# Loads, engines and a new written-out order for the first groups of an attention and mixture-of-experts kernel

## The chip, the cores and the metric

One core of a Trainium2 chip runs the whole program: TensorE (PE), VectorE (DVE), ScalarE (ACT), GpSimd (POOL) and the DMA queues that SyncE (SP) and ScalarE issue. The metric is device microseconds of one launch. Three runs of the kernel before took 917.5, 918.54 and 920.09 us, median 918.54 us; the execution that was profiled took 916.3 us.

## The reference

`q`, `k` and `v` are 8 batches of 12 heads, 448 tokens of 64 elements each, in f32. Attention output is turned to 3584 tokens of 768 and goes through a mixture of 8 experts.

```python
q_n = q / sqrt(mean(q*q) + 1e-6) * g_q          # k_n likewise with g_k
scores = q_n @ k_n.T / 8
attn = softmax(scores)                          # the row maximum subtracted first
x = (attn @ v) as [3584, 768]
logits = x @ w_gate                             # then tokens to experts, greedily by logit, 448 each
out[tokens of e] = relu(x[tokens of e] @ w1[e]) @ w2[e]
```

## The kernel before

The 96 heads are worked in 24 groups of four heads. A group is 14 blocks of 128 rows for q and as many for k. Every f32 value that TensorE multiplies is split into a high and a low f16 half, so that a product is three matmuls.

For a group g the steps, by the names of the functions that the profile's lines belong to, are: load q and k (`load_qk`, lines 227 and 235 for the first three groups, 252 for the others); square on ScalarE (`square`, L301); sums of squares on VectorE (`sumsq`, L307); 1/sqrt in three steps (`rsqrt`: Ln on ScalarE, L313; Exp on ScalarE, L315; then a correction called the root, on VectorE in three small operations, L324 to L326, or on GpSimd in four, L318 to L321); q times the product of the two gains (`gain`, L368 or L371); q and k times 1/sqrt (`norm`, L342); the high half (`hi`, ScalarE, L376); the low half, value minus high half (`lo`, L379); transposes of both halves; a first product of high halves for the row maxima (`max_score`, L504 and L507, TensorE, and `max_reduce`, L514, VectorE); the maxima turned into a row (`put_max`, `rows_first`, `row_first`, L520 to L432); the scores (`scores`, L535 to L544), exp (L550, ScalarE) and attention times v (`av`, L569).

Groups 0 and 1 (`EARLY = 2`) go half by half, a = 0 (blocks 0 to 3) and a = 1 (blocks 4 to 6), and are transposed on TensorE (L402) and copied out of PSUM by VectorE (k's part, L410) and ScalarE (q's part, L412). From group 2 on a whole group goes at once and a DMA transposes it (L389). The tables `FIRST` and `ENG` say which engine does a step: "D" is VectorE, "P" GpSimd; a key such as `normk1` holds for half 1 of that group alone.

`load_qk(0, n)` for group 0: n = 0 to 3 is q, n = 4 to 7 is k. Parts 0 and 4 bring 192 KB (first heads of each pair), 1, 2, 5 and 6 bring the 32 KB tails, and 3 and 7 the other 192 KB. Half 0 needs the first three of these, half 1 the fourth. `load_qk(1, n)` and `load_qk(2, n)`: 0 to 2 is q (384 KB and two tails), 3 to 5 is k. Loads of group 0's k go on ScalarE's queue, all others on SyncE's. DMAs share eight completion semaphores: in the trace the first eight DMAs take one each, and each later one waits for the DMA that last had its semaphore.

What order the work has: `plan()` makes a list of 2117 tasks of the attention stage, each with its engine, and `ORDER` is a table of two characters for each task, written out, in which `Plan.run` emits them. Every engine and queue works through its own tasks in that order and waits where an operand isn't there. The routing and the experts come behind it and don't use the table.

Of the kernel before, what the change touches and what calls it, by code (L numbers as in the profile page):

```python
# [89 lines left out]
class Attention:  # L90
# [789 lines left out]
    def plan_first(self, plan, g, a):  # L880
# [51 lines left out]
        "3V3Y3W3X3a3bC7ROC83rME2S2q2T2r4A2sMGC9MF2UH5CACBCCRPMKH7CDCEMJMHMICF4BCG3s4C3tH6H83G2u2v202w1-2tRQRRH9HBHA3c4Y"
        "4ZCHCIHDRSHCHE3Z3d3u3w3v4a3y3H0D3I3JCJCKMLMNMRCL4DCM3x3+4E4F3KHFHGHHHICNCORTRUMMMOMQCPCQRV4cRW3z0E3-403L4G4HMP"
        "HJCRCSHL4KHKHMMSCTMTMYMWMX4dCUCVHN4bHOCWRXRYHPHQ3e3fMUCXRZCYHRMVCZ4eRaHS4fRb4I4L4J4M3gHVHTCaCbRc0FCcRd4NReMZMb"
        "MdCdHUHWRfCeRgMaHX4y4+CfCgMfMgMjCh4zCiMmMeMi4g4h414k4-Mc4O5K3lCjCkRhRiHZ5L4i4j4l3h3jHY3kHa4m3i0G4nHb4243444P4o"
        "MkClRjRkCmMhHd50HcCnRlCoMl4546He51525453RmRnHfCpCqRoHh4748HgHiMnCrRpCsHj4p49HlCtMsMtMrCuRqRvRuRyCvCwHkHm5M5O5N"
        "HnHpCxCyHo5PMoMpMqMu4Q4RS3Hr56HqHsCzS4C+11MyMvM+C-D0S5HtHxD1D2554S6658595A57MzMxMw4TD35QHu5RS65kS7S8S9D4SAHvHw"
        "Hy5mM-N5D5N4N3D6HzD75lD8N2H-4qSB4VSC4rH+I05n5o5p5S5T4U5W5U5V4WI15YI2D9DAN6N1N7NCDBDCN0SDI3I4685q5ZDDSEDESFNANB"
        "N8DFDGI5SGI6SHI7DHDIN9SISJRxRr67Rw5X5r5sI9DJDKSKI8IA5B4sIBICSLRzR+R-DLDMSMID6AIF5uIEIGRs5a4X6u6vDNDO69S0S15t5v"
        "4tNDNENH5C5DS2IHDPDQ6BNFNKNMDRNINGDS5w6W5xII6C4v4w6D6E6F4u6GIJDVNJILIKIMDWDTDUSNSOSPSQNNNPNQDXINIO5E5bIPIQDYDZ"  # L940
        "DaSRNLIR5yDbDc6X6H6I6K6LNONRNUNTSSSTRt4x5J5F6JIS5cIT5dSUSVDdDeSWNXIVDfNWNYNeDgNdDhNbNSNV5H6Y6ZIU6w6a6b5IIW5z6c"
        "6d5eDiDjSlSmDkSn5GIXIYIZDlDmSoSp6e6f0HNZNaNcDnIbIaSbSaId6gIc6yIe5f6hDo6xSqSr5+5-SsStNfNjNi6MDpDqIfIg5hIhDr6z7I"
        "6+6-70Ii6i6j72735g0I0JDsSuNlNgNhNkDtSvDuIjIkSc5jSdSeSfSgShSwSxSyDvDwIl7KImInSzDxSi5iSjDyNmNsNoDzNnNpNrNq7LD+D-"
        "S+S-E0Sk7g6k606NSXIp6l616462710KIoIrE1E2T0IqIsNtNuNw6O6P7JT1T2ItE3E4NyNxNvNzT3747M767N7O77757P7QN+O0E7T4E8T5Iv"
        "IuIwT6IxIy63E5E6O3N-O1E9T7EAIz65I+I-EBECO2O4T87RJ07iJ1T9TA6R6S6TJ2TBEDEEO5O7O66mTC6n7j7S6QJ3J47h6U7k78J5EFEGOC"
        "OEO8EHJ7O97UJ67V7TEIJ87l7mOAOBJ9EJSZ6VSYTHTI6oTK7WTRTSTTEK7nTUTVJBJAJCODOHENEOJDJF8486JEELEM85JGOJOGOOOIEPEQ87"
        "JHJIJJEROPOLESOFTWTXTYJL7A7BJK7o7q7p797sJNETEU7r7u7t0L7vTZJMJO8889TaTJ8S8T6p8A6s8B8C6qOMOKONTbTcEVEWTdJPJQ6rTL"
        "TNTMEXEYTeTfJRJTJSEbEcTOOQOVOUEZ8U8VEaJUTPTQ6t7CJXJVEd8D8W8s7XJW8E8GTGTE7w8IJY8FEeOXObOWEfOROTOdOS7D7EEg8X8Y8u"
        "8Z7GEhTgEiThJZJb7Y7ZTiOcEjEk8a8H8c8bJaTjJcTkOZOYOaTlElTmEmTn8vJdOeOgEnOjOkOhOfOiEo7FToJe7x8e8d8g8h8fTF7H7bTpEp"
        "TqTrEqJfJgJh7f7a9ETDErEsTsOlOrOnEtOqOoOmEu7yJiTtTu7zJj8t7+7c7e9GJkJlEvJm8w0M0NOsOpEwU79HOuOvExJnJoJpEyU8U97d8x"  # L950
        "UAJqEzOyE+UBOtOwOx0O8yE-UCF0UDUEJrJt9F9IJsJuUFF1F2OzP0O+P1F3UGF4JvJx8z8i8JTzU0T-T+83F5F68+8-0P9e9fJwJy0Q0R7-80"
        "9092P2O-P4P98K8L8MTx9JJz819KJ+J-F7F8P8P3P5P7UHUIUJK0UK9LF9FAULK1K3FBFC919M9NA0TyP6PA8N938O9OK2K49g8PU1U3U2UMUN"
        "UOFDFEK5K7UP82UQFFU4K6U5K8FGPBPEPGPHPDU69h9i9j9P8jFHFIPIPCPOFJA2A1A49QFKA3K98Q948RKAKB9SKCFLPFFMPNPJPLFNURUSUT"
        "UUFOKDKF8kUV8lTv958m9U9R8r9T0S0T0U0VPMPKUWUX0W0X8n8pKEKG8o9k0Y0Z0aFRFS0b9lKHKJKIKKFPUYFQPPPQPVFTFUKLKNUZUaUfUh"
        "KMFVFWPUPWPYFXKPKOKQFYKRKSFZFaPZKT8qKU96KV97TwUi9mKW9oAQ9nFbFcPcPXPSFdFeKXKYKZKa9qFhFiPRPTUpUqUrPaFfFg98KdKbUs"
        "UtFjFkPb9D9r999p9CKcKeA5UuUvA6A79BA80cAAABA90dPdPhPiPgFlKfKgFmUwUxKhKi9sFnFoUyPePjPfUz9W9XU+KjU-V0FpUgUjUlUkKl"
        "FqV1FrARFsUmPkPpPqPoPmUnUoFtFu0e9APrPnPwFvPxASATFwPlV29VACAEAF0fAD0gAoAq9YApAGV3V4AUAVAWKkKm9Z9aAXPsPtFxFyKn9d"
        "Uc9tV5V6KoKpFzF+PvPuV7Kr9uV8V99v9wUbUdAH9bKq9cKsKtF-ArG0PyQ2Q0P+G1AsVAVBKuG2KvKxG3G4AaKwAY0h0i0jAZAc0k0lKyAeUe"
        "Q1P-PzQ30mVCAtG5G6KzK+Q7Q9VDVEG7G89x0n0oAd0pAu9zVFAv9+VGVKVHK-L0AwAbAf9-VLVM9yL1L2BCBEAxAyAzG9GAQ5Q6QAQGGBGCBF"
        "L3L5L4GDGEQBQ8Q4QEQFVVVWVXL6VYAIL7L9L8AJAKAPVOGFBD0qVZQDGG0r0sQHQCALVaBGA+BHLAB0AOQIQJGHVbVcGILBLDVdVeLCLEGLGM"  # L960
        "QLQMQKGJGKAMA-BIBJB1BK0tQOQNQRQPGNLFLHVfVgVhViGOGPGQVjQTQQQUQSVkVlBMLGLIB2GRGSLJLLAgAhVmLKLMVNVPVRVQGTVJAiBLGU"
        "AjVnANVoLNBOLOAmLPLQGVGWVSQVQWQZGZGaLRLSVTLTGXGYQaQXQbVUGbGcLVLULWLXAlLYGdQYQcQiQhGeVpVqVrB3AnBQGfGgLZLbB4VsLa"
        "B5VtVIB6LcQgQfQeQdVuVvVwVxVyV-W1W3W2W4AkQjQnQkGhLd0u0vBN0w0x0yLeLfQmQoLgGiGjGkLjLhLiGnGoQpQlWBWCWDQqQrGlGmLkLl"
        "LnGpGqQuQwQsGrB7B9BAWEWFGsLmLoLpLrLqBSQtBTQvWJWKB8QxR0QyR1Q-Q+QzBPBRW0BUV+VzBBWLLtWMWSWTWNLsLuWULvW5W7W6LwWVWW"
        "BVLzLxX3W8W9WABYLyL+BXR2R6R7R3R5R4R8L-M1WGM0M2WaWbWcWdWeM5M3M4WHM6BWR9RFRERARCRBRGRLRKRJRDRMRIRHWjWkWlWrWsWtWm"
        "WnWOWQWuWPWXWfWhWYWvWIW-X0WRWxWoWZWgWiX1WpWqX2W+WyWzWw"
# [1031 lines left out]
```

## Time and profile before

| | us |
|---|---|
| median of three runs | 918.54 |
| profiled execution | 916.3 |
| its span, first to last instruction | 914.5 |
| PE busy in the span | 863.1 |
| DVE busy | 660.6 |
| ACT busy | 466.9 |
| POOL busy | 343.0 |

The profile page lists busy time by engine, a strip of 40 slices, the chain of work that ended last, and the costliest groups of instructions. The trace answers further questions: busy time of each engine in any stretch, waits by engine and releaser, and the instructions of a stretch in order of time.

### The profile page before, as it was taken

What the parts mean: (1) busy time and instruction counts of PE and PEld (TensorE: products, weight loads), DVE (VectorE), ACT (ScalarE), POOL (GpSimd) and SP (SyncE); (2) the same over time, 40 slices, a digit from 0 to 9 for tenths busy, and PEclk for the clock granted to TensorE, in tenths of its full rate; (3) what the DMA queues carried; (4) which work ended last, traced back from release to release, by engine and by line L of the source; (5) the groups of instructions that cost most, each with busy time, mean ns of one, the idle gap of its engine ahead of it and who ended that gap; (6) DMA issues with size and microseconds to landing.
All of it is one profiled execution on the core that took longest, in us unless ns stands there. A gap on an engine that the chain in (4) does not pass through costs nothing.

```text
span 914.5 us, 30177 instructions
## 1 busy us (share of the span) xinstructions
PE 863.1 (94%) x13219; PEld 579.4 (63%) x13220; DVE 660.6 (72%) x1465; ACT 466.9 (51%) x670; POOL 343.0 (38%) x433
## 2 busy tenths in 40 slices
...
GB/s 198 113 157 173 183 261 156 219 179 224 205 230 182 210 203 143 114 82 63 253 86 251 182 190 268 150 282 91 298 88 282 142 219 258 155 130 69 131 18 44
DMA packets 224952, 157.31 MB, mean 172 GB/s; under 512 B 162100, under 2 KB 211508, under 8 KB 224820
## 3 DMA queue, kind: packets, MB, share of 16 engines
...
q8 instruction: 103, 1.69, 0.7%
q10 hardware_dynamic: 834, 0.46, 0.2%
...
## 4 chain that ended last, share of the span: by engine, by line
PE 71%; issue 17%; DVE 5%; POOL 3%; DMA 2%; ACT 1%; SPq 1%; POOLq 0%; DVEq 0%
PE po L569 18%; PE ph L1775 16%; PE py L1792 13%; PE psc L535 9%; PE pm L504 4%; PE psc L537 3%; PE py L1801 2%; DVE mx L514 2%; POOL out_dram L1808 1%; POOL rows L1712 1%; DMA kqh<-s 1%; PE psc L542 1%; PE rp L1318 1%; DVE st L307 1%; PE rp L1475 1%
## 5 line engine op out<-in xcount | busy, mean ns | idle before, releaser
L514 DVE TENSOR_REDUCE mx<-pm 128x2 f32<-128x896 f32 x162 | 176.7, 1091 | 49.2 <-PE pm L504 44.8
L569 PEld LDWEIGHTS po<-v,e 128*64 128x64 f32 x5376 | 166.8, 137 | 31.8 <-issue 28.9
L569 PE MATMUL po<-v,e 128*64 128x65 f32 x5376 | 182.6, 223 | 2.9 <-issue 2.8
L1775 PE MATMUL ph<-xt,w1h 128*128 128x448 f16 (+2 forms) x708 | 183.5, 343 | 0.4 <-DVE xt L1733 0.3
L550 ACT ACTIVATE e<-psc 128x896 f32<-128x896 f32 x168 | 148.6, 912 | 49.9 <-PE psc L537 39.3
L1808 POOL DMA_INDIRECT out_dram<-y,idx x32 | 34.4, 1075 | 307.9 <-ACT y L1794 279.3
L1792 PE MATMUL py<-w2h,hh 128*128 128x384 f16 x384 | 125.0, 326 | 0.0
L1792 PE MATMUL py<-w2h,hl 128*128 128x384 f16 x384 | 125.0, 326 | 0.0
L1792 PE MATMUL py<-w2l,hh 128*128 128x384 f16 x384 | 125.0, 326 | 0.0
L1775 PE MATMUL ph<-xt,w1l 128*128 128x448 f16 (+2 forms) x354 | 119.9, 343 | 0.0
L1792 PEld LDWEIGHTS <-hh 128*128 128x128 f16 x768 | 73.6, 97 | 45.6
L1775 PEld LDWEIGHTS <-w1h 128*128 128x128 f16 x708 | 64.7, 97 | 52.7 <-issue 1.5
L1764 ACT ACTIVATE hh<-ph 128x448 f16<-128x448 f32 x56 | 30.5, 544 | 125.8 <-PE ph L1775 122.7
L1794 ACT ACTIVATE y<-py 128x384 f32<-128x384 f32 x48 | 23.5, 490 | 116.2 <-PE py L1792 96.0
L1712 POOL DMA_INDIRECT rows<-xd,idx x32 | 31.0, 969 | 114.9 <-DVE idlo L1480 46.8
L1579 DVE SCALAR_TENSOR_TENSOR w2l<-stage,w2h 128x768 f16<-128x768 f32 x64 | 60.2, 951 | 8.6 <-ACT w2h L1575 8.6
L504 PE MATMUL pm<-kqh 64*64 64x448 f16 x588 | 56.7, 362 | 1.8 <-DMA kqh<-s 1.4
L535 PE MATMUL psc<-kqh 64*64 64x448 f16 x588 | 56.0, 353 | 0.8 <-issue 0.4
L537 PE MATMUL psc<-rowq,rowk 64*64 64x448 f16 x588 | 55.8, 349 | 0.7 <-issue 0.7
L1766 DVE SCALAR_TENSOR_TENSOR hl<-ph,hh 128x448 f16<-128x448 f32 x56 | 34.1, 617 | 30.9 <-ACT hh L1764 30.8
L307 DVE TENSOR_REDUCE st<-sq 128x14 f32<-128x910 f32 (+2 forms) x52 | 52.7, 1016 | 4.4 <-ACT sq L301 4.4
L535 PE MATMUL psc<-kql,kqh 64*64 64x448 f16 x588 | 55.4, 349 | 0.0
(301 smaller groups left out, 1620.8 us busy)
## 6 DMA issues: line engine op xcount, KB each, us to landing
...
```

What stands on the lines that cost most here:

```text
L307: self.nc.vector.tensor_reduce(self.stat(g, 0, a)[:, i], self.view(self.T["sq", g, i], a), axis=AX.X, op=OP.add)
L504: self.nc.tensor.matmul(o, mine, self.every(k, r, a), start=True, stop=True)
L514: self.nc.vector.tensor_reduce(m, p[r, :, :448], axis=AX.X, op=OP.max)
L535: mm(o, mine, self.every(q, r, n), start=i == 0, stop=False)
L537: mm(o, one[r, :64], self.every(row, r, n), start=False, stop=True)
L550: self.nc.scalar.activation(e, p[:, :, :448], AF.Exp, scale=scale)
L569: self.nc.tensor.matmul(po[o:o + 64, w], self.T["e", d][:, h, q:q + 64], self.v32[g % 2][:, h, 4 * a + d % 7 % 4], start=d == ds[0], stop= ...
L1579: self.later(0.93, lambda w=w: self.nc.vector.scalar_tensor_tensor(l[:, w], v[:, w], self.WS, h[:, w], op0=OP.mult, op1=OP.subtract), k, i)
L1712: nc.gpsimd.indirect_dma_start(out=g[:n, c, :], out_offset=None, in_=self.xd, in_offset=bass.IndirectOffsetOnAxis(ap=idx[:n, c:c + 1], axi ...
L1775: nc.tensor.matmul(p, a, b[:, o], start=st, stop=sp)
L1792: nc.tensor.matmul(p, a[:, f, s], b[:, f, o], start=st, stop=sp)
L1808: st = nc.gpsimd.indirect_dma_start(out=self.out, out_offset=bass.IndirectOffsetOnAxis(ap=self.router.out[k][:n, c:c + 1], axis=0), in_=y[ ...
```

## The change

Three entries of `FIRST` and the whole table `ORDER` are replaced.

```diff
-    FIRST = (dict(root="D", gain="P", normq="P", normk="D", normk1="P", lok="D", lok1="P", loq="D", loq1="P"),
-             dict(root="D", gain="P", normq="P", normk="P", lok="P", loq="P"), dict())
+    FIRST = (dict(root="D", gain="P", normq="P", normq0="D", normk="D", normk1="P", lok="P", loq="P"),
+             dict(root="P", gain="P", normq="P", normk="P", lok="P", loq="P"), dict())
     ORDER = (
-        "050204031506160z1718191A0+1B0708000-1C1E1G1c1F1H1d1I1J1e1K1f1L091g1h1i1N1D1b1M011P1R242122252326281k1j1O1Q2x2z"
...
+        "03060402010507080z151618170+000-1D191A1B1C1E1F1c1d1G1H1e1I1J1f1K1g1h1i091L1N1b1k1j1n1l1p1O1M1P1R1o1Q1m21232624"
...
```

In group 0 the low halves of half 0 (k and q) go from VectorE to GpSimd, and q's norm of half 0 goes from GpSimd to VectorE. In group 1 the root of both halves goes from VectorE to GpSimd: three operations on VectorE become four on GpSimd, for each half. All else keeps its engine. The two tables, decoded by task number, begin so for each engine (x.y is group and half, h and l high and low half, "max 3.0" a block of the first product):

```
SP before:   q0 part 0, part 1, g_q, part 2, part 3, k1 main, q1 main, q1 tail, k1 tail, q1 tail, k1 tail, q2 main, ...
SP after:    g_q, q0 part 0, part 1, part 3, part 2, q1 main, q1 tail, k1 tail, k1 main, q2 main, k3, k1 tail, q1 tail, k2 main, q3, ...
ACT before:  load k0 part 4, 5, g_k, part 6, part 7, square q0.0, k0.0, q0.1, rsqrt 0.0 (2), square k0.1, rsqrt 0.1 (2), hi k0.0, hi q0.0,
             square q1.0, hi q0.1, square k1.0, hi k0.1, square q1.1, copy h0.0, ...
ACT after:   load g_k, k0 part 4, 5, 6, 7, square q0.0, q0.1, k0.0, k0.1, rsqrt 0.0 (2), rsqrt 0.1 (2), hi k0.0, hi q0.1, hi k0.1, hi q0.0,
             square q1.0, q1.1, k1.0, copy h0.0, copy h0.1, square k1.1, ...
DVE before:  ident, gains, sums q0.0, k0.0, q0.1, root 0.0, sums k0.1, norm k0.0, mask, root 0.1, lo k0.0, lo q0.0, copy h0.0, sums q1.0,
             k1.0, q1.1, copy l0.0, root 1.0, sums k1.1, max 0, max 1, root 1.1, copy h0.1, max 2, sums q2, max 3.0, ...
DVE after:   ident, gains, sums q0.0, q0.1, k0.0, k0.1, root 0.0, root 0.1, mask, norm k0.0, norm q0.0, sums q1.0, copy h0.0, sums q1.1,
             copy h0.1, sums k1.0, k1.1, max 0, max 3.0, max 2, copy l0.0, max 1, sums q2, copy l0.1, max 4, sums k2, row 0.0, ...
POOL before: gain 0.0, 0.1, norm q0.0, q0.1, k0.1, lo q0.1, k0.1, gain 1.0, 1.1, norm k1.0, q1.0, lo k1.0, norm q1.1, k1.1, lo q1.1,
             q1.0, k1.1, root 2, norm q2, k2, gain 2, lo k2, lo q2, ...
POOL after:  gain 0.0, 0.1, norm q0.1, k0.1, lo k0.0, q0.1, q0.0, k0.1, gain 1.0, 1.1, root 1.0, root 1.1, norm k1.0, q1.1, q1.0, lo q1.1,
             norm k1.1, lo q1.0, k1.0, root 2, lo k1.1, norm q2, k2, gain 2, lo k2, lo q2, ...
PE before:   transposes h0.0, l0.0, max 0, 1, 3.0, transposes h0.1, l0.1, max 2, 4, transposes h1.0, rows 0.0, max 3.1, 6, transposes h1.1, scores 0
PE after:    transposes h0.1, h0.0, max 3.0, 0, transposes l0.0, l0.1, max 1, 2, 4, rows 0.0, max 3.1, 6, transposes h1.0, max 5, scores 0
```

Further on the two tables hold the same tasks in nearly the same places on TensorE: the first score block of each group, counted in TensorE's 748 tasks, stands within eight places of where it stood. The DMA queue and GpSimd differ more. Of the 22 groups that a DMA transposes, the number whose high half is issued in the table with no reduction to spare before the first block that reads it is 11 before and 2 after.

## Rows read from the trace of the kernel before

**Rows 1.** Stretches: us; PE, PEld, DVE, ACT, POOL busy; clock; DMA share; GB/s.

```profile
0.00:19.30 19.30, 2.81 (x18) 1.95 (x18) 9.52 (x22) 8.55 (x18) 10.78 (x32) 1.00 0.72 203
19.30:45.00 25.70, 18.60 (x192) 10.01 (x194) 24.19 (x33) 19.04 (x39) 20.59 (x23) 1.00 0.41 118
...
100.00:400.00 300.00, 294.94 (x7547) 226.38 (x7541) 236.72 (x366) 220.60 (x326) 196.91 (x228) 1.00 0.96 194
```

**Rows 2.** What PE waited for, 0 to 60: us in total, times, longest.

```profile
PE po L402 <- ACT s L376: 9.5, 1, 9.5
PE pm L507 <- DVE mx L514: 5.9, 6, 3.0
```

**Rows 3.** First loads in order of time: start, us, engine; idle before in brackets.

```profile
4.06 0.46 SPq L235 DMA_DIRECT2D qkraw<-in_k_dram  x1
...
4.75 0.60 ACTq L227 DMA_DIRECT2D qkraw<-in_k_dram  x1
...
6.12 0.63 ACT L301 ACTIVATE sq<-qkraw 128x512 f32<-128x512 f32 x1 [4.10 <-issue]
...
10.04 1.05 ACT L301 ACTIVATE sq<-qkraw 128x512 f32<-128x512 f32 x2 [3.29 <-DMA qkraw<-in_k_dram]
```

**Rows 4.** Data rate in the first stretches, columns as in rows 1.

```profile
0.00:5.00 5.00, 0.08 (x1) 0.11 (x1) 0.51 (x2) 1.28 (x1) 3.17 (x23) 1.00 0.42 108
5.00:10.00 5.00, 0.58 (x2) 0.39 (x2) 0.92 (x2) 0.63 (x1) 2.22 (x2) 1.00 0.98 272
```

**Rows 5.** First group's operations in order of time, columns as in rows 3.

```profile
12.01 0.18 DVE L324 TENSOR_TENSOR st<-st 128x16 f32<-128x16 f32 x1
...
12.99 1.35 DVE L342 TENSOR_TENSOR kn<-qkraw,st 128x512 f32<-128x512 f32 x1
...
15.04 0.69 DVE L379 TENSOR_TENSOR s<-kn,s 128x512 f16<-128x512 f32 x1
...
15.12 1.30 POOL L342 TENSOR_TENSOR qn<-qn,st 128x384 f32<-128x384 f32 x1 [1.15 <-DVE st L326]
...
15.65 1.32 DVE L379 TENSOR_TENSOR s<-qn,s 128x512 f16<-128x512 f32 x1
...
18.65 0.60 ACT L412 ACTIVATE kqh<-po 128x512 f16<-128x512 f16 x1
...
19.30 0.59 PE L507 MATMUL pm<-kqh 64*64 64x448 f16 x4 [1.68 <-ACT kqh L412]
```

**Rows 6.** Second group's roots on DVE beside POOL, columns as in rows 3.

```profile
19.36 2.23 POOL L368 TENSOR_TENSOR qn<-qkraw,gg 128x512 f32<-128x512 f32 x2
...
19.64 1.02 DVE L324 TENSOR_TENSOR st<-st 128x16 f32<-128x16 f32 x1
...
22.21 1.08 DVE L514 TENSOR_REDUCE mx<-pm 128x2 f32<-128x896 f32 x1
```

**Rows 7.** Groups by line and shape, 0 to 60: busy, mean ns, idle before.

```profile
L379 POOL TENSOR_TENSOR s<-kn,s 128x512 f16<-128x512 f32 x1 | 1.2, 1154 | 0.0
```

**Rows 8.** Third group on POOL in order of time, columns as in rows 3.

```profile
31.51 0.23 POOL L318 TENSOR_TENSOR st<-st 128x28 f32<-128x28 f32 x1 [1.39 <-ACT st L315]
...
32.78 1.69 POOL L342 TENSOR_TENSOR qn<-qkraw,st 128x896 f32<-128x896 f32 x1
...
39.73 1.89 POOL L379 TENSOR_TENSOR s<-kn,s 128x896 f16<-128x896 f32 x1 [1.58 <-ACT s L376]
```

**Rows 9.** Third group's first DMA transpose and its first reader, columns as in rows 3.

```profile
40.51 1.48 SPq L389 DMA_TRANSPOSE kqh<-s  x1
...
46.83 0.38 PE L507 MATMUL pm<-kqh 64*64 64x448 f16 x4
```

**Rows 10.** Same four matmuls early and later on PE, columns as in rows 3.

```profile
36.21 0.58 PE L542 MATMUL psc<-kqh 64*64 64x448 f16 x4
...
39.62 0.38 PE L542 MATMUL psc<-kqh 64*64 64x448 f16 x4
```

**Rows 11.** What PE waited for, 60 to 410, columns as in rows 2.

```profile
PE pm L504 <- DMA kqh<-s: 1.4, 1, 1.4
```

More of the change, by code (lines that the diff above doesn't have):

```diff
@@ L927 @@
     ORDER = (
-        "050204031506160z1718191A0+1B0708000-1C1E1G1c1F1H1d1I1J1e1K1f1L091g1h1i1N1D1b1M011P1R242122252326281k1j1O1Q2x2z"
-        "2-2y302+123M3N1n2A1o1l1m2W1U1S292B1TBZ2X2C2D1V2Y1W2E312ZBa2a2bBbBf1pBc2c1sBd1qBe32272V2F2G2H331u2I2e2d2J1rBh2h"
-        "2f2i2K2g2L3OBg1X1Y1t342MBi2N353637BnBl14131z1Z1aBo2jBm2kGtGuBj2OBkBp39383ABqGvBr3Q2l3RBs1v1wGwBv3B3C3D3E0A1+3m"
-        "3n0B0C1x1yBw2P2m2o2QGxBtGzGyX4G+Bu3P3S3o3q3TBxByG-H0BzB+M7MDMAM83p3F10C3C4MCC1C2B-H1H2C02R2pH3C52nC6M9MBRN3UH4"
@@ L932 @@
[L932 to L966, printed above, removed]
+        "03060402010507080z151618170+000-1D191A1B1C1E1F1c1d1G1H1e1I1J1f1K1g1h1i091L1N1b1k1j1n1l1p1O1M1P1R1o1Q1m21232624"
@@ new lines @@
+        "2x3N25222+272V282W292A1S2X1q2B1TBf1r2Y2Z2aBZBaBg2C2D2E1U1sBbBdBe1VBc2b2c2F2e3M122y1+302-20142z3132332H2h1uBh1X"
+        "1W1Y1tBi2G2J3435361Z1aBnBoBlBm2L2MBjBk2i2d2K2I37Gt2O3O2NBp2f3PBvBq2g39383A2jBw2PGu1v2Q1-13101z2l3Q1wBr1yGvBs1x"
+        "3BGw3D3m0A3C3EBtBu2k2mGxGyGzG+3R3S3oBxC1ByC2BzM7MAMCM83pB+3T3U3W3V3n3FG-C3MBC4H12R2tH0B-C02nH33qX4H22o2pH4C5C6"
+        "MDM9RNROC7C83rME2S3X3Y3a2u2w3G2v3c4Y2T2q2s2rMFC9MJ2UCAH5CBRPCCMIH7CDCE4A3s3tRQH6H83b3ZMKH93u3v4C3yHACFCGRRMHHB"
+        "HCCHCIMG3KRSRTHD3H3I3d3L3J4Z3w3x3+3-40HE3z4DMLCJMPMMMRCKRURVCLCM4BHFHGHHHI4E4F4G4I4HCNCORWMNMOMQRXRYCPCQRZHJHL"
@@ new lines @@
+        "4aCRCSMSMVMUCTMXMYMWHKRa4bHM4c4J0B0C4yCU4dCVCWHNHP3e3fCXCY4e4fHO4gRbHR4K4LHQHS4M4NMTRc413g5K4OCZCa3h3k3j4h4iHT"
+        "HVCbRdHUCcReMZMfMbCdCe0D0E4jRfHWRgMdHXHYCfCgMaMeMcChMgMjMiMm4zCiCj4+3l4P4-50514k524lRhCkHZHb42RiHa43MkClMhRjCm"
+        "HdRkHcHeCnRlCoMl453i53Hf4mHgCpRmRnRoCqHhMnMpCrHj445L4oRpHiHkRqRrCsRsRvRw4nHlHm5M47Ct0FCu0G54MoMtMsCvCw11HnHpCx"
+        "55565OHo5758Cy5NMuMwMyMx4QHr4R495A4S664pRy5PHq5QHs485RCzMrMqMzMvC+C-S3S4S5D0HtHxD1S6M+S7D2HuHv5S5kD3S8D4S9SAHw"
+        "HySB46M-N4N2D5D6N5Hz595U5V4TH+D7SCD8H-N64q4r5B4XRx5m5nI1D9DAN0N35lI05T0H5W5Y5o4W5p5X4U5a5q5rI3DBDCNBN1NCSDSEDD"
@@ new lines @@
+        "DESFI2I44VSGN8N7NADFDGI5I7I6I8DHSHDIN94tSI5Z5s5tI95uDJDKSJSK4sIBIAICSLRzR+R-DLDMSMIFID68DNS0IES1DOS24wIGNDNE5C"
+        "675w6A4v5x5v5D5ENINJDPNGNF69IHDQDRNKIJ6B6WIIIKDSDVDWNN6XILDTDUNPNMNLNHSNSODXDYINIM6C6DSP4x6uRuIPDZDaIOSQSRNONQ"
+        "SSIR5y5bRt5z6E6G4u5J6vDbDc6YIQ6Z6FNRNSNTNV5cNX5dSTSU6IISSV5F5G5I6H6K6w6a6b6M5e0I6L6J6c6eDdDeSWSbScSdSeITIVIUIW"
+        "6yDfDgNWNYNbDhNcNUNdDiDjIXIYIZSlSmDkSnDlDmSoSpNZNeNaIa5H5jDnDo6xSqIb6NIdIcIe6d6g6f0J0K0L5+5-NfNiNlDp6zDqSrSsIf"
+        "IhDrDsIg0M6i6kStSuNhNgNjNkSvDtDuIjIi5f5i6j5g5h6+6-Ik706h71SYSfSgShSwSxSyDvDwInIlSzDxDySi7IIm7KSjIo7JNmNrNqDzD+"
@@ new lines @@
+        "NoNnNsNpS+SkD-E0IpIqSZ60SX7g747h656lItE1S-T0E2T1NtNyNvNwNz6O6PT27273766Q786175637762IrIs7L64Iu7M7i7NE3E4NxNuN+"
+        "O2O3O1T3T4T5T6E7E8IvIxIwE5O0IzIy7k6VE67O7Q7P0N0O0P7RE9I-N-O46R6SI+J0T7EA7lEBECJ179J37SJ27U7VJ4EDO5O6O9J5EE7j7m"
+        "6mT8T96nTAJ7EFEGOAOBO87WSaJ66U7nTBTC6oTHTDTFTJTITKEHEIJ9J8JAJBEJEKOCO7OIOHTRTSTTENEO84JC86TUTVJFJDELEM7o0Q7q7r"
+        "7T0R0S0T7p0U6TJEJG8785OEOJODOPOKOLEPEQJHJJERESOFOOOG6p6q7s7u6sJI7w7X7v0V0W7ATW7B7C8S8TTXTYJLJKJMTZETJN88JOEUTa"
+        "ONOMEVEWTbTcTdJP89JQJREXEYTLTMTNTeTfJTEbTOOQOVOWEcEZEa8A7t0XJSJUTPTQ6t8CJXJV6r8U8B8E7H8DEdEe8VJW8WOSOTOXOUEfEg"
```

18 lines of the change are left out of this document (added).

## The prediction

> **What bounds the kernel now.** I read the stretches first. In 100 to 400 us TensorE is busy 294.94 of 300 us, so there the attention stage ends when TensorE has done its work, and only 5.06 us of idle time are to be had [rows 1]. What is left to win lies at the start: TensorE is busy 2.81 of the first 19.30 us and 18.60 of the next 25.70 us, that is 16.5 and 7.1 us idle [rows 1]. After that it is saturated, so time won before 45 us should reach the end of the stage nearly whole.
>
> Next, the waits say who holds TensorE back there: 9.5 us for ScalarE's first cast, which is the end of the load, square and norm chain, and then 5.9 us in six waits for VectorE's maxima [rows 2]. VectorE is busy 24.19 of 25.70 us in that second stretch [rows 1]. So there are two bounds in a row: the first group's chain up to the first product at 19.30 us [rows 5], and then VectorE.
>
> The order of time shows how the chain starts late. ScalarE squares q at 6.12 us and then waits 3.29 us, until 10.04, for k of half 0 [rows 3]. That k's second tail is issued by ScalarE's queue at 4.75 us only, behind a 384 KB load of the second group that SyncE issued at 4.06 us (one of two) [rows 3].
>
> **The change, part by part.**
>
> Loads. In the new order g_k stands first on ScalarE's queue and k's four loads behind it; on SyncE's queue one 384 KB load (q of group 1), not two, can come ahead of the last piece of k. Each gain row moved to the front costs the loads behind it one issue, about the 0.5 to 0.6 us of the issues shown [rows 3]; it is hidden as long as ScalarE is still issuing, since its first square can't start before its fifth issue ends, as at 6.12 us now. Bytes that must move before k's half 0 is there: q of group 0 0.46 MB, half of k 0.26, q of group 1 0.39, together 1.11 MB. The rows give 108 GB/s over the first 5 us, 0.54 MB, and 272 GB/s after [rows 4]: 5 + 0.57/0.272 = 7.1 us. Both squares of q stand ahead on ScalarE: 6.12 + 0.63 + 0.5 = 7.25 us [rows 3]. I take 7.3 us for k's square, against 10.04. The ends are 7.25 (ScalarE not free earlier) and 10.04 (nothing won).
>
> From k's square to the first product. Now 2.95 us pass from k's square to the norm of k (10.04 to 12.99) [rows 3, 5]. The new order puts the root of half 1 ahead of it, three operations of 0.18 [rows 5]: the norm starts at 7.3 + 2.95 + 0.55 = 10.8 and ends 1.35 later, at 12.15 [rows 5]. Behind it ScalarE does four casts, three squares of group 1 and then the copy that the first product needs. Four of the seven are 512 wide and take 0.63 like the square [rows 3], three are 384 wide, three quarters of it, some 0.5: 4.0 us, so the copy starts at 16.15, takes 0.60 [rows 5] and the first product starts at 16.8. It is at 19.30 now: 2.5 us won.
>
> The norm of q's half 0, new on VectorE, is not shown there. The nearest rows are 1.35 for k's norm beside GpSimd and 0.69 for a low half of that size without it [rows 5]; I take 1.35, since GpSimd works on half 1 at that time. It ends at 13.5, before ScalarE comes to its cast (the last of the four), so it is hidden there.
>
> The page SBUF — State Buffer of the Trainium skill, section "SBUF: two separate sides", says that VectorE with two inputs and GpSimd take a shared port in turn, one blocked for the whole instruction of the other. By that rule the norm would take up to 1.30 + 0.69 = 1.99 us instead of 1.35; the cast of q would still find it done by 14.2 and the sum stays, so I go by the row.
>
> VectorE up to its first reduction. Now this is at 22.21 us, with group 1's root of half 0 ahead of it; its first operation takes 1.02 us beside GpSimd's gain instead of 0.18 [rows 5, 6]. In the new order the last thing ahead is the sum of k's half 1 of group 1. Its square is two ScalarE operations (0.5 each) behind the copy that ends at 16.75, so it is ready at 17.75, the sum takes about 0.5, and the first reduction starts at 18.3: 3.9 us earlier. The other root, which now stands between reductions, goes as well; by the first, 1.02 + 2 x 0.18 = 1.4 us at most. VectorE's lead is thus 3.9 to 5.3 us. That two low halves leave VectorE (0.69 and 1.32 [rows 5]) and a norm comes (1.35) is in this chain already.
>
> GpSimd. It gets two low halves of 1.15 us [rows 7] and two roots of 1.27 each (31.51 to 32.78, the group 2 root [rows 8]), 4.8 us, and loses one norm, about as long as the norm of half 1, 1.30 [rows 5]. It now goes from the norm of q's half 1 at 15.12 [rows 5] to the norm of group 2 at 32.78 [rows 8], 17.66 us, in which it waits 1.39 us for a root [rows 8]. In the new order it starts at 10.6 (the root of half 1): 10.6 + 17.66 + 4.8 - 1.4 = 31.7 us when the wait goes, 33.1 when it stays. So group 2 is 1.1 us early to 0.3 late on GpSimd, and a further 1.58 us of waiting ahead of its low half of k [rows 8] may go. What is late next would be group 2's transpose: issued at 40.51, first read at 46.83 [rows 9]. Even with the issue of 1.48 us and as much again for the landing, some 3 us lie between. A lead of 3.5 us on TensorE eats this room and no more, so I cost GpSimd at nothing, though with little cover.
>
> The GPSIMD Engine Reference of the Trainium skill, section "Engine selection", speaks against this part: elementwise work with two inputs is about twice as slow on GpSimd and belongs on VectorE. The rows agree where VectorE is alone (0.69 against 1.15) and not beside GpSimd (1.32) [rows 5, 7].
>
> The sum. Before the first product 2.5 us are won. Of the 7.1 us that TensorE idles behind it, VectorE's shorter list gives back some: 1.4 us more lead at the first reduction (3.9 against 2.5), of which I take 1.0, since TensorE must also catch up its own work. Together 3.5 us; ends 2.5 and 5.3. The stretch to 400 us I leave as it is: same work, nearly the same order on TensorE. Its ends are the 1.4 us wait for a transposed tile that may vanish [rows 11], and the present 5.06 us of idle twice over.
>
> The profiled execution takes 916.3 us and its span 914.5; 3.5 off gives 912.8. The median of the runs stands 2.2 us above the profiled execution, so I forecast 918.5 - 3.5 = 915.0 us.
>
> **The rivals.**
>
> GpSimd becomes the bound. For it: the 4.8 us that it gets, and only some 3 us of room at group 2's transpose. Against: TensorE waits nowhere for it now [rows 2]. Then the lead of group 2 counts, -0.3 to 2.7 us: about 1.2 us won, 917.3 us.
>
> The start shrinks to what can't be hidden. q's tail of group 1 is issued behind loads of groups 2 and 3, and ScalarE's square of it stands ahead of the copy that the first product needs. With 2.6 MB ahead it lands at 5 + 2.06/0.272 = 12.6 us; it is wanted at 14.4. Each us later than that is lost whole. The other way to lose is TensorE's pace: four matmuls take 0.58 us at 36.21 and 0.38 at 39.62 [rows 10]; if the pace doesn't rise earlier with the work, 3.5 us more of it run at the slow pace, 3.5 x (1 - 0.38/0.58) = 1.2 us lost. Then 2.3 us are won: 916.2 us.
>
> The change doesn't do what it says: k's last piece still waits for a completion or for bytes, and its square stays at 10.04. Then the first product isn't earlier, and only VectorE's 1.4 us of roots are won: 917.1 us.
>
> Slower: late transposes in the full stretch. The DMA engines are at a share of 0.96 over 100 to 400 us [rows 1], and the table is new there too. Mechanism: SyncE's queue works in order, so one transpose behind a store or a load that isn't ready comes late, and TensorE waits 1.4 us as it did once [rows 11]. 22 groups are transposed so. From three of them the 3.5 us are gone; from five the kernel is slower than the bound of what can be told; with six it is 918.5 - 3.5 + 8.4 = 923.4 us. Against it: the new table issues most of them with more room (two without any, eleven before).
>
> **How the numbers follow.** A measurement of this kernel tells about 0.3%, 2.8 us, from no change. Chances: the forecast, 2.5 to 5.3 us won and up to 1.4 more, 0.55; GpSimd 0.12; the shrunken start 0.13; not what it says 0.08; slower transposes 0.12. Faster by over 0.3%: nearly all of the forecast and a little of the shrunken start, 0.55. Within: GpSimd, most of the shrunken start, the fourth, and transposes where few are late, 0.34. Slower: 0.11. The low end is 5.3 + 1.4 = 6.7 us won, 911.8; the high end is one beyond which lies about the slower case, 919.8. The forecast's own range is 912 to 916.
>
> **What would show it.** k's first square near 7.3 us, not 10; the first product near 16.8; the first reduction near 18.3, with no root on VectorE behind group 1's sums; group 2's transpose issued near 37 to 39; TensorE's idle time in 19 to 45 us under 7.1 us, and in 100 to 400 near 5. I am wrong if TensorE's idle time before 45 us has not shrunk by at least 2.5 us, or if that in 100 to 400 us has grown by as much.

## The result

The changed kernel takes 924.3 us (median of 17 runs, 919.49 to 930.36), the kernel before on the same chip 917.68 (17 runs, 913.86 to 922.59): a ratio of 1.0067, interval 1.0048 to 1.0086. It is slower; 915.0 was forecast, and 924.3 lies outside the range, 911.8 to 919.8.

| | before | after |
|---|---|---|
| profiled execution, us | 916.3 | 927.6 |
| its span, us | 914.5 | 925.8 |
| k's first square | 10.04 | 7.64 |
| first product | 19.30 | 17.43 |
| VectorE's first reduction | 22.21 | 18.92 |
| TensorE busy in 100 to 400 us | 294.94 | 286.55 |

### The profile page after: what moved, and what is told of

It reads as the page before. It is cut to its first block, busy times and chain, and to the rows that moved or that the text cites. A ratio compares the mean times of both kernels' runs of the same rounds, so it can differ in the third digit from the quotient of the medians.

```text
span 925.8 us, 30182 instructions
## 1 busy us (share of the span) xinstructions
PE 865.5 (93%) x13219; PEld 581.7 (63%) x13220; DVE 657.4 (71%) x1458; ACT 466.9 (50%) x670; POOL 345.6 (37%) x442
## 4 chain that ended last, share of the span: by engine, by line
PE 72%; issue 17%; DVE 5%; POOL 3%; ACT 2%; DMA 1%; POOLq 0%; SPq 0%; DVEq 0%; ACTq 0%
PE po L569 18%; PE ph L1775 15%; PE py L1792 13%; PE psc L535 9%; PE pm L504 4%; PE psc L537 3%; PE py L1801 2%; PE psc L542 1%; POOL out_dram L1808 1%; DVE mx L514 1%; POOL rows L1712 1%; PE rp L1318 1%; PE rp L1475 1%; DVE st L307 1%; ACT sq L301 1%
## 5 line engine op out<-in xcount | busy, mean ns | idle before, releaser
L569 PEld LDWEIGHTS po<-v,e 128*64 128x64 f32 x5376 | 168.7, 138 | 36.7 <-issue 34.3
L569 PE MATMUL po<-v,e 128*64 128x65 f32 x5376 | 184.7, 224 | 3.6 <-issue 3.6
L379 POOL TENSOR_TENSOR s<-qn,s 128x896 f16<-128x896 f32 (+2 forms) x26 | 45.7, 1758 | 29.7 <-ACT s L376 26.3
```

Of the source, the lines that this page charges most:

```text
L379: self.tt("lo" + name, g, a)(self.half(g, 1, name, a), self.flat(self.T[name + "n", g], a), self.half(g, 0, name, a), op=OP.subtract)
L569: self.nc.tensor.matmul(po[o:o + 64, w], self.T["e", d][:, h, q:q + 64], self.v32[g % 2][:, h, 4 * a + d % 7 % 4], start=d == ds[0], stop= ...
```

## The profile after

The same stretches as in [rows 1]: us; PE, PEld, DVE, ACT, POOL busy; clock; DMA share; GB/s.

```profile
0.00:19.30 19.30, 4.20 (x32) 3.08 (x33) 9.22 (x23) 9.65 (x21) 13.38 (x35) 1.00 0.83 234
19.30:45.00 25.70, 17.10 (x205) 9.51 (x204) 21.23 (x26) 18.02 (x37) 20.65 (x29) 0.80 0.36 99
100.00:400.00 300.00, 286.55 (x7197) 218.45 (x7193) 231.18 (x343) 214.92 (x317) 196.49 (x228) 0.99 0.90 190
```

TensorE idles 13.45 us in the full stretch instead of 5.06, and in the second stretch its clock is 0.80 of full. Up to VectorE's first reduction the start did what was forecast; these rows, in order of time, answer to [rows 3, 5, 6, 8, 9]:

```profile
7.64 0.63 ACT L301 ACTIVATE sq<-qkraw 128x512 f32<-128x512 f32 x1 [0.35 <-DMA qkraw<-in_k_dram]
...
11.99 1.32 DVE L342 TENSOR_TENSOR qn<-qn,st 128x512 f32<-128x512 f32 x1
...
17.44 0.94 PE L507 MATMUL pm<-kqh 64*64 64x448 f16 x4
...
18.92 1.08 DVE L514 TENSOR_REDUCE mx<-pm 128x2 f32<-128x896 f32 x1
...
32.52 1.68 POOL L342 TENSOR_TENSOR qn<-qkraw,st 128x896 f32<-128x896 f32 x1
...
40.75 1.65 SPq L389 DMA_TRANSPOSE kqh<-s  x1
```

The lead of 3.3 us at the first reduction is gone at the third group's transpose (40.75, before 40.51 [rows 9]). What TensorE waits for in 0 to 60 us says where; ScalarE's order is shown under it:

```profile
PE pm L507 <- ACT rowq L430: 2.8, 1, 2.8
PE psc L423 <- ACT qm L520: 2.7, 1, 2.7
PE pm L507 <- DVE mx L514: 1.6, 2, 1.2
```

```profile
35.56 1.06 ACT L461 ACTIVATE v<-vraw 128x1024 f32<-128x1024 f32 x1
36.52 0.47 ACT L412 ACTIVATE kqh<-po 128x384 f16<-128x384 f16 x1
36.89 0.94 ACT L301 ACTIVATE sq<-qkraw 128x896 f32<-128x896 f32 x1
37.73 0.52 ACT L430 ACTIVATE rowq<-pm 1x448 f16<-1x448 f32 x1
38.16 0.93 ACT L376 ACTIVATE s<-kn 128x896 f16<-128x896 f32 x1
```

The maxima cost 1.6 us instead of 5.9 [rows 2], but two waits for ScalarE have taken their place: its row copy stands behind a copy of v, a copy and a square. TensorE's clock is at half (1.2 GHz) in 24.7 to 31.5 us and, behind the wait of 2.8, in 38.4 to 41.8.

Behind the start, what PE waited for in 60 to 412 us; "issue" is a stall that no semaphore shown ends:

```profile
PE pm L504 <- issue: 5.1, 2, 3.5
PE po L569 <- issue: 3.6, 6, 1.0
PE po L666 <- issue: 1.5, 1, 1.5
PE pm L444 <- DVE mx L514: 1.2, 1, 1.2
PE psc L535 <- ACT e L550: 1.0, 1, 1.0
PE psc L537 <- issue: 0.9, 1, 0.9
PE psc L535 <- issue: 0.6, 1, 0.6
```

No wait for a transposed tile is among them; the one of [rows 11] is gone. The longest stall on PE, and the queue of SP ahead of it:

```profile
146.17 0.35 PE L504 MATMUL pm<-kqh 64*64 64x448 f16 x3
150.03 0.35 PE L504 MATMUL pm<-kqh 64*64 64x448 f16 x1 [3.51 <-issue]
```

```profile
136.56 0.37 SPq L252 DMA_DIRECT2D vraw<-in_v_dram  x1
137.02 0.72 SPq L252 DMA_DIRECT2D qkraw<-in_q_dram  x1
137.79 0.52 SPq L620 DMA_DIRECT2D xd<-xa  x1
138.41 6.64 SPq L389 DMA_TRANSPOSE kqh<-s  x1
```

I first took this for the transpose of group 9, issued at 138.41 and landed at 149.8. It is not: the stall stands between the third and the fourth of four matmuls of one product, that product is the last of group 8 (the ninth group), and group 9's first one starts at 153.19. The page says what else moves on the DMA engines (queue, kind: packets, MB, share):

```profile
q8 instruction: 103, 1.69, 0.7%
```

103 packets of 16 KB, and TensorE's recorded weight loads and matmuls are 26,439: some 257 for each packet. So I take them for blocks of TensorE's own program; 128 spare instructions of TensorE (half_after, below) make them 104. Counted by its recorded instructions, the nine stalls of over 0.45 us without a releaser between 45 and 412 us stand here:

```
stall starts, us   74.0  119.3  146.5  186.2  192.1  231.2  236.0  277.3  318.8
length, us         0.67   0.94   3.51   1.05   1.56   0.47   0.95   0.62   1.49   sum 11.25
block landed       73.2  118.6  147.6  185.8  192.3  230.2  235.5  276.4  319.0
instruction        1727   3773   5051   6839   7095   8885   9139  11185  13227
(n-1727)/255.5     0.00   8.01  13.01  20.01  21.01  28.02  29.01  37.02  45.01
```

All nine stand at a border of blocks, and TensorE goes on 1.3 to 2.4 us behind the landing of a block. The kernel before has three such stalls (instructions 2495, 4029, 15017; 3.01, 9.01 and 52.02 on the same scale), 2.66 us together; they are among these waits, of 60 to 412 us:

```profile
PE po L569 <- issue: 2.8, 5, 1.3
PE psc L537 <- issue: 0.7, 1, 0.7
```

The longest stall and the one at 318.8 each have a stretch of half clock behind them, 151.0 to 154.4 and 321.7 to 325.1 us. The first is seen here, by windows with columns as above, and by two rows of TensorE in it and behind it:

```profile
150.00:151.20 1.20, 1.17 (x27) 0.89 (x28) 0.78 (x1) 0.00 (x0) 0.00 (x0) 0.91 1.23 309
151.20:154.60 3.40, 3.40 (x52) 2.00 (x50) 1.68 (x4) 1.87 (x2) 2.62 (x2) 0.53 1.02 248
154.60:158.00 3.40, 3.40 (x96) 2.83 (x96) 2.88 (x6) 0.51 (x1) 0.39 (x2) 1.00 0.77 285
```

```profile
152.07 0.58 PE L535 MATMUL psc<-kqh,kql 64*64 64x448 f16 x4
157.31 0.36 PE L535 MATMUL psc<-kqh,kql 64*64 64x448 f16 x4
```

A product of four matmuls follows the last after some 0.38 us in the stretch at half clock and after 0.19 behind it, so 3.4 us at half clock lose at most 1.7. The profiled pair lies 11.3 us apart, and the terms are late blocks 11.25 - 2.66 = 8.6, half clock at most 3.4, waits of over 0.45 us for other engines and transposes 2.27 - 1.45 = 0.8: 12.8 at most. How much of the distance lies where can be read off. TensorE's first 1010 matmuls are the same set in both kernels, and the next one starts at 82.1 us before and at 81.9 after, so the whole lead of the start has shrunk to 0.2 us there. The last matmul of the attention stage ends at 410.8 and 421.8 us, and what comes behind takes 503.8 and 504.1. So the loss lies between 82 us and the end of the attention stage.

The Trainium skill, page "Runtime: NRT & Kernel Launch", section "Instruction fetch mechanics", says that an engine's program comes in blocks of 16 KiB, 256 instructions, over a DMA queue of its own, and that crossing a border is mostly hidden. The size agrees with the 257 above. The cost does not: 0.47 to 3.51 us at nine borders.

## Experiments

All ran in 5 rounds beside the kernel before, 6 to 12 runs each (the change itself 17); ratios compare with the kernel before of the same rounds. The last four columns, in us, are of the one profiled run: "late blocks" the sum of stalls of over 0.45 us at borders without a releaser, 45 to 412 us; "half" the half clock between 60 and 400 us; the span; and the end of the attention stage's last matmul.

| kernel | median us | ratio to before, interval | late blocks | half | span | attention ends |
|---|---|---|---|---|---|---|
| before | 917.3 to 919.3 | 1 | 2.66 | 0 | 914.5 | 410.8 |
| after | 924.3 | 1.0067 [1.0048, 1.0086] | 11.25 | 6.8 | 925.8 | 421.8 |
| first_only | 920.98 | 1.0027 [1.0003, 1.0050] | 4.31 | 0 | 915.7 | 411.6 |
| order_only | 927.04 | 1.0094 [1.0059, 1.0129] | 9.05 | 3.4 | 923.2 | 419.1 |
| new_start | 917.97 | 0.9997 [0.9971, 1.0023] | 5.38 | 0 | 916.5 | 412.2 |
| old_start | 924.47 | 1.0084 [1.0056, 1.0112] | 4.71 | 3.4 | 922.1 | 414.8 |
| sp_old | 942.79 | 1.0275 [1.0246, 1.0305] | 5.31 | 13.7 | 940.1 | 436.0 |
| sp_new | 937.05 | 1.0210 [1.0173, 1.0247] | 6.92 | 13.7 | 935.7 | 431.9 |
| trh9 | 922.33 | 1.0045 [1.0023, 1.0066] | 4.93 | 3.4 | 917.3 | 413.1 |
| start_row | 917.30 | 0.9994 [0.9974, 1.0014] | 2.71 | 0 | 915.5 | 411.5 |
| mended | 923.01 | 1.0061 [1.0034, 1.0088] | 7.89 | 13.7 | 928.4 | 424.4 |
| light_after | 910.76 | 0.9914 [0.9892, 0.9935] | 0.47 | 0 | 910.3 | 406.2 |
| light_before | 909.51 | 0.9916 [0.9888, 0.9943] | 0.52 | 0 | 907.5 | 402.5 |
| half_after | 918.60 | 1.0001 [0.9981, 1.0020] | 7.11 | 0 | 918.8 | 414.2 |
| quarter_after | 928.58 | 1.0106 [1.0070, 1.0143] | 9.87 | 0 | 925.1 | 419.4 |
| half_before | 922.44 | 1.0045 [1.0021, 1.0068] | 7.11 | 0 | 920.8 | 412.4 |
| half_trh9 | 920.65 | 1.0026 [1.0002, 1.0049] | 5.78 | 3.4 | 919.4 | 415.2 |
| half_row | 921.16 | 1.0011 [0.9986, 1.0037] | 9.85 | 0 | 924.7 | 415.1 |

Two more, pad_after and pad_before, are told below; their starts were delayed.

Behind the attention stage most of these runs need 503.8 to 505.0 us; quarter_after needs 505.8, old_start 507.3, half_before 508.4 and half_row 509.5. In these four the first product of an expert is late by 1.34 to 3.99 us, here in old_start and in half_before:

```profile
574.77 0.54 PE L1775 MATMUL ph<-xt,w1h 128*128 128x448 f16 x2 [2.97 <-issue]
571.97 0.91 PE L1778 MATMUL ph<-xt,w1h 128*128 128x448 f16 x2 [2.97 <-issue]
```

This stall has no releaser either, but it is no late block: it stands at instruction 21363 in old_start and, with 64 and 128 spare instructions ahead, at 21427 and 21491, so it goes with the work and not with the borders. In pad_after, where it takes 5.03 us, the profile names the transpose that brings xt. What these four spans lose there lies behind the stage that the tables order.

**Which part: engines, order, start or the rest.** first_only has the three new entries of `FIRST` with the old `ORDER`, order_only the reverse. new_start takes the whole change up to the first score block of the third group (some 60 us) and the old table behind it, old_start the reverse.

```diff
 # new_start: ORDER =
+tasks of the new table up to score 14, in its order
+all other tasks, in the order of the old table
```

> The engines of the change (low halves, q's norm, group 1's roots) with the old table. Theory, late transposes behind the start: within 1 us of the kernel before, since the table is the old one. Rival, the start or the engines: about 6 us slower, as the change is.

> The new table with the old engines. Theory: about 7 us slower than before, since the new table is there. Rival, the engines cost: within 1 us of before.

> The change up to the first score block of group 2 (some 60 us), the old table behind it. Theory: the new start gives no more than 1 us by then, and the old rest adds nothing: 0 to 1 us faster than before. Rival, the start spoils the rest: 5 us or more slower.

> The old table and engines up to the first score block of group 2, the new table behind it. Theory: 6 to 8 us slower than before, as the change is. Rival, the start: within 1 us of before.

By the medians the loss lies in the new table behind the start: old_start has it whole, 1.0084, and new_start has none, but no gain either. (In old_start's one profile the attention ends only 4.0 us later than before; another 3.5 us of its span lie behind that stage.) The engine moves alone cost 0.3%, more than the 1 us expected, by an interval that nearly reaches no change.

**SyncE's queue alone.** sp_old is the change with the old order of SyncE's tasks behind the start; sp_new is the kernel before with the new one.

```diff
 # sp_old: ORDER behind score 14
-SP's tasks in the order of the new table
+SP's tasks in the order of the old table; all others as in the new one
```

> The change, but SyncE's queue behind the start in the order of the old table; all other engines in the new order. Theory, the DMA queue's order makes transposes late: the loss goes, 916 to 919 us. Rival, the order on the compute engines: it stays at about 924.

> The kernel before, but SyncE's queue behind the start in the order of the new table (one load of v moved ahead by two places). Theory, the DMA queue's order: about 6 us slower than before. Rival, the compute engines' order: within 2 us of before.

Both miss by far: 942.79 and 937.05 us. A queue in the order of one table starves the computing order of the other (12.3 and 12.0 us of TensorE's waits have a releaser here, against 2.27 in the change), so these two tell nothing of which is better.

**One transpose, one row copy.**

```diff
 # trh9, SP:                          # start_row, ACT:
+high transpose of group 9           +row copy of group 0, half 1
 v of group 7                         copy h0.1 / v / copy / square
 q of groups 12 and 13, 896 KB       -row copy of group 0, half 1
 store of x
-high transpose of group 9
```

> The change, with group 9's first transpose issued ahead of a load of v, a 896 KB load of q and a store instead of behind them. Theory, that transpose is late behind those bytes: the wait of 3.5 us at 150 us and the slow clock behind it go, 3 to 4 us faster than the change. Rival, its input is late: no difference to the change.

> new_start with ScalarE's copy of the first group's second maxima row put ahead of two copies of turned halves, one of v and one square. Theory, that order on ScalarE costs TensorE 2.8 us at 38 us and the clock behind it, where the new start's lead is lost: 2 to 3 us faster than new_start, 915 us. Rival, VectorE's order holds the start: no difference to new_start.

trh9's median is about 2 us below the change, less than the 3 to 4 expected, and the two intervals (1.0023 to 1.0066, 1.0048 to 1.0086) overlap, so a gain is not shown. The stall of 3.51 us is gone from its profile. As the position of that stall shows, this does not make it a wait for the transpose: what was moved behind it also stood ahead of the block. Its profile has no half clock before 60 us either, though its start is that of the change. start_row equals new_start (917.30, 917.97): the half clock moved to 40.6 to 47.4 us, and no time came of it, against the 2 to 3 us expected.

**Are the stalls blocks of the program?** Spare matmuls behind the one that spreads the gains, where TensorE idles, move every border against the work.

```diff
             nc.vector.tensor_copy(self.gg, p)
+            p = self.po_tile()[:, :64]
+            for _ in range(64):
+                nc.tensor.matmul(p, one, gq, start=True, stop=True)
```

> The changed kernel with 64 spare matmuls (128 instructions of TensorE, each weight load counted) right behind the one that spreads the gains, where TensorE idles; nothing else differs. Theory of code blocks: TensorE's instructions come in blocks of 16 KB, 256 instructions, over the same DMA engines as the data (the profile counts 103 packets and 1.69 MB of a queue called instruction), and the nine stalls of the changed kernel that no semaphore ends (11.25 us together from 45 to 412 us, the longest 3.51 us in the midst of four matmuls of a first product) are blocks that come late behind data. Then every border moves by 64 matmuls, some 3.3 us of work: the stall of 3.51 us in the ninth group's product is gone from that matmul, new ones lie 64 matmuls earlier or nowhere, and their sum becomes what a random place gives, 3 to 8 us (the profiles so far have 2.7 to 11.3), so about 919 us. Rival, late transposes: the stalls belong to the order of the DMA queue; they stay at the same matmuls with the same sum, and the time stays at 924.

> The kernel before with the same 64 spare matmuls at the start. Theory of code blocks: the three stalls that no semaphore ends (2.66 us from 45 to 412 us; the largest 1.31 at 124.0 us) go from their matmuls, others come 64 matmuls away; the sum was among the lowest seen, so it rises to 3 to 8 us and the time by 1 to 5, to about 920. The wait of 1.45 us for the seventeenth group's transpose stays. Rival, late transposes: the same stalls at the same matmuls, 917.5 to 918.5.

A failure of design: in f32 each of these is two passes, 256 instructions, so the borders fell on the same matmuls again, and the spares kept TensorE busy until 32 us. 940.22 (938.34 to 947.19) and 933.62 us (930.36 to 937.35) are the price of a late start. Seven stalls at borders stay in pad_after, 5307 = 5051 + 256 and 7351 = 7095 + 256 among them.

```diff
+            p = self.po_tile()[:, :16]
+            for _ in range(64):          # quarter_after: 32
+                nc.tensor.matmul(p, one.bitcast(F16)[:, :128], gq.bitcast(F16)[:, :16], start=True, stop=True)
```

> The changed kernel with 128 spare instructions of TensorE (64 f16 matmuls of 16 columns and their weight loads), half a block, at the start; the spare f32 matmuls of before were two passes each, 256 instructions, a whole block, so the borders stood at the same matmuls again. Theory of code blocks: counted from the first instruction the stalls that no semaphore ends stay on the grid of 255.5, so against the work they lie 64 matmuls earlier: none is left at the fourth matmul of the ninth group's product, nor at the other eight; their sum is drawn anew, 3 to 8 us against 11.25, and with it the time: 917 to 922. Rival, the stalls belong to the order of work and of the DMA queue: same matmuls, 10 us or more, 924.

> The changed kernel with 64 spare instructions of TensorE at the start, a quarter of a block. Theory of code blocks: the stalls lie 32 matmuls earlier in the work than in the changed kernel, some 1.5 us; those that stood behind a long queue of data shrink or grow by up to 1.5 us, the sum 4 to 11 us, time 918 to 924. Rival: same matmuls, same sum, 924.

> The kernel before with the same 128 spare instructions. Theory of code blocks: its sum of 2.66 us was a lucky place; half a block on it is 3 to 8 us, and the stall of 1.31 us at 124.0 us goes from its matmul: time 918 to 923. Rival: same matmuls, 2.7 us, 917.5 to 918.5.

Here the spares take 1.90 us and end at 6.94, long before TensorE has work. In half_after the stalls are at instructions 5051, 7095, 9907, 11441, 13483 and 13737 (13.01, 21.01, 32.02, 38.02, 46.01, 47.01 on the scale): borders again, two of them (5051 and 7095) the same as in the change, but other work. At number 5051 there is now attention times v (PE in order of time, lines 3 higher than before):

```profile
140.56 0.36 PE L507 MATMUL pm<-kqh 64*64 64x448 f16 x4
140.85 1.38 PE L572 MATMUL po<-v,e 128*64 128x65 f32 x39
143.91 0.92 PE L572 MATMUL po<-v,e 128*64 128x65 f32 x25 [1.68 <-issue]
144.76 0.38 PE L507 MATMUL pm<-kqh 64*64 64x448 f16 x4
```

The stall that stood in the product is 64 matmuls earlier, and halved. The waits for VectorE and ScalarE, which are of the order, stay to the tenth (60 to 412 us):

```profile
PE po L572 <- issue: 7.7, 8, 1.9
PE pm L447 <- DVE mx L517: 1.2, 1, 1.2
PE psc L538 <- ACT e L553: 1.0, 1, 1.0
```

128 spare instructions that compute nothing take the change from 924.3 to 918.6 us, level with the kernel before; the intervals of the two ratios don't meet. The kernel before goes from 918.2 to 922.4, but in its profile the attention stage ends only 1.6 us later (412.4, before 410.8), and 4.6 us come behind it, with the expert's late product, so this rise is not shown to be of the blocks. A quarter of a block makes the change 928.58, more than its range allowed; its interval and that of the change overlap. That the stalls are of the program's blocks is shown; that a given border is good or bad is not foreseen.

**Is it the data that makes them late?** The loads of q and k from group 6 on are left out.

```diff
     def load_qk(self, g, n):
+        if g > 5:
+            self.T["raw", g // 2] = self.T["raw", 2]
+            return
```

> The changed kernel without the loads of q and k from group 6 on (18 of 896 KB; the groups behind compute with the data of groups 4 and 5), everything else in its place. Theory of code blocks: with the DMA queue light, blocks come in time: the stalls that no semaphore ends fall from 11.25 us to under 2 from 45 to 412 us, none over 0.7, though each border is at the same matmul; no half clock between 60 and 400 us; time 912 to 915. Rival: they are something of TensorE itself (a change of the kind of matmul, a write to a bank), and stay at the same matmuls with 8 us or more; time 921 to 924.

> The kernel before without the loads of q and k from group 6 on (the groups behind compute with the data of groups 4 and 5). With the blocks in time in both kernels (0.5 us of such stalls in the changed one without these loads, which took 910.8), the time that the change wins at the start should now be seen. Theory of code blocks with the forecast's start: the kernel before without these loads takes 912.5 to 915, 2 to 4 us more than the changed one so. Rival, the new table is worse behind the start by itself or the start wins nothing: 908 to 911, the same as the changed one or less.

Stretch and waits for light_after, then for light_before:

```profile
100.00:400.00 300.00, 296.81 (x7600) 228.03 (x7598) 236.37 (x359) 224.06 (x332) 197.05 (x229) 1.00 0.78 150
...
PE pm L447 <- DVE mx L517: 1.2, 1, 1.2
...
PE psc L538 <- ACT e L553: 1.0, 1, 1.0
PE po L572 <- issue: 0.8, 2, 0.5
```

```profile
100.00:400.00 300.00, 298.92 (x7698) 230.45 (x7690) 236.02 (x368) 222.12 (x329) 195.11 (x227) 1.00 0.79 149
...
PE po L572 <- issue: 0.5, 1, 0.5
```

With DMA at 0.78 to 0.79 instead of 0.90 to 0.96 the late blocks all but vanish in both, and light_after lies below the 912 to 915 us expected. And then the change is not faster: 910.76 (910.16 to 912.17) against 909.51 us (908.93 to 914.37), so the forecast of 2 to 4 us for the start fell, its rival held. In the profiled pair the attention stage of the change ends 3.7 us later (406.2 and 402.5): 1.3 of these are there behind the first 1010 matmuls (81.8 and 80.5), and the two waits of 1.2 and 1.0 us in light_after are of the new table. So late blocks are not all that the new table costs.

**Can it be mended?**

```diff
 # mended = trh9, and:                            # half_trh9, half_row:
 SP:  k of 14, 15 behind high transpose of 12     trh9, start_row with 128 spare
 SP:  k of 22, 23 and a store behind that of 20   instructions as in half_after
 DVE: split of the gate's weights behind 2 maxima
 ACT: copy of v of group 11 behind 2 exps
```

> The change with group 9's high transpose ahead of three transfers, as run before, and five more tasks moved: k's 896 KB load of groups 14 and 15 behind the high transpose of group 12, k's load of groups 22 and 23 and one store of x behind the high transpose of group 20, the splitting of the gate's weights (2.7 us on VectorE) behind the next two maxima, and one copy of v on ScalarE behind two exps. Theory of code blocks: the stalls of 2.11 and 2.03 us at 183.6 and 309.6 us come from blocks that stand behind two such loads at once; with the loads apart both go, with them the half clock behind the second (3.4 us at half, 1.7 lost), and the two real waits of 1.22 and 1.04 us go with the tasks that made them. Span 917.3 less 4.1, 1.7 and 2.3: 909 to 912, time 913 to 917, faster than the kernel before. Rival, late transposes: neither stall was a wait for a transpose of its group, the loads moved come later themselves; 921 to 924, as with the one transpose moved (922.3).

> The change with group 9's high transpose ahead of three transfers, and half a block (128 instructions) of spare matmuls at the start. Theory of code blocks: moving one transpose and moving the borders are both draws of where a border meets a long queue, so the two gains (2.0 and 5.7 us on the changed kernel) don't add up; the sum of stalls that no semaphore ends is 3 to 8 us again and the time 916 to 922. Rival: a late transpose and a late block are two causes; both go, stalls under 3 us, 914.5 to 916.5, faster than the kernel before.

> The new start with the row copy moved, on the old table behind it (917.3 us, stalls that no semaphore ends 2.71 us), with half a block of spare matmuls. Theory of code blocks: its place was a lucky one like that of the kernel before; moved by half a block the sum rises to 4 to 8 us and the time to 919 to 923, as it did with the kernel before (918.2 to 922.4). Rival: what the half block cost the kernel before was chance of that table alone; 916.5 to 918.5, same as without.

mended failed: the blocks that came late at 183.6 and 309.6 us in trh9 came in time, and others came late instead, 2.52 us at 274.3 and 1.87 at 183.4, 7.89 in all; the waits that it was to remove went, and others of 1.93, 1.60 and 2.49 us for ScalarE came. Its time is in the rival's range. In half_trh9 (expected 916 to 922) the gains of two causes don't add up to the rival's 914.5 to 916.5, and stalls of 5.78 us stay. half_row lies where the theory of blocks put it, but its interval also holds no change, and 5.5 of the 9.2 us by which its span exceeds start_row's come behind the attention stage, so it decides nothing. No version with all its loads is faster than the kernel before.

## Why the prediction was wrong

**The step that failed** is the one put as "The stretch to 400 us I leave as it is: same work, nearly the same order on TensorE". Its upper end, the idle time of 5.06 us twice over, was too low as well: 13.45. It was read as a stretch that waits for little; that TensorE's program itself comes over DMA engines at a share of 0.96 [rows 1], and that stalls without a releaser stood in the waits before (2.8 and 0.7 us above), was not weighed. In place of a stretch that stays as it is the runs showed late blocks of 11.25 us instead of 2.66 and, behind two of them, 6.8 us at half clock. The kernel before has the lowest sum of the full kernels profiled; that its borders stand well by luck is the likely reading, from one profile each.

**The second** is that time won before 45 us "should reach the end nearly whole". TensorE's idle time before 45 us was 45 - 21.42 = 23.6 us and is 45 - 21.30 = 23.7: my own condition for being wrong. ScalarE took over as the bound (2.8 and 2.7 us), and 10.2 us went at half clock. new_start, with the old table behind, and light_after, nearly without late blocks, show the same. Of the 3.5 us, 0.2 were left behind the first 1010 matmuls. In trh9, which has the same start and neither half clock nor a late block up to there, the next one starts at 80.0 us, so even then 2.1 would be left.

**A reference that was late.** The start before was read from one execution. Five profiles have that start, and their first product stands at 17.68 (light_before), 18.25 (old_start), 18.87 (sp_new), 18.92 (half_before) and 19.30 us; eleven with the new start and no delay have it at 17.25 to 17.87. The 2.5 us that the forecast won there were measured from the latest of the five.

**What held.** k's square 7.64 (7.3 forecast), first product 17.43 (16.8), first reduction 18.92 (18.3), q's norm on VectorE 1.32 us (1.35) and hidden, group 2's norm on GpSimd 32.52 (31.7 to 33.1). GpSimd did not become the bound. Group 2's transpose, 40.75, missed 37 to 39, for ScalarE's order. One reading behind this does not hold: the 0.69 us taken as a time without GpSimd ran from 15.04 to 15.73, and GpSimd's norm is on record from 15.12 to 16.42; the operation of 1.32 behind it starts inside that norm [rows 5]. So these rows show no VectorE operation alone and leave open whether the two engines take turns. The sum did not depend on it.

**The slower rival** had the amount, 923.4 us, and not the mechanism: TensorE waited for no transpose in the full stretch of the change.

**What stays open.** Executions of one kernel spread by up to 11 us (the change 919.49 to 930.36), and the late blocks are known of one each, so the sums explain spans roughly, and only up to the end of the attention stage: of the 4.8 us between the spans of old_start and trh9, 3.1 lie behind it. Which transfer delays which block, what the expert's late product depends on, and whether quarter_after is slower than the change at all, was not settled.
